# Retention on quarters of the PE array: chunks of 64 tokens, stages batched over 512

## The chip, the cores and the metric

One core of one Trainium2 chip. The time is the device time of one launch in microseconds (us), medians over runs in the undisturbed state. All times inside a kernel come from the profiled run and count from the start of its span, which is 1.7 to 2.2 us shorter than the device time. PE is TensorE, PEld its weight loads, DVE is VectorE, ACT ScalarE, POOL GpSimd, SP the engine that issues the DMAs.

## The reference

```python
def _attn_ref(q, k, v):            # (B, H, S, D) = (4, 8, 768, 64), fp32
    gamma = 1.0 - 2.0 ** (-5.0 - np.arange(H))
    for t in range(S):
        state = gamma * state + outer(k[:, :, t], v[:, :, t])     # D x D per head
        y[:, :, t] = q[:, :, t] @ state / sqrt(D)

def _moe_ref(x, w_in, w_out):      # x: 3072 x 512, w_in: 512 x 2048, w_out: 2048 x 512
    h = x @ w_in
    g = np.where(h > 0, h, np.exp(np.minimum(h, 0)) - 1)          # ELU
    return g @ w_out
```

Retention first, then a two-layer network over its output. The network is most of the work. The kernel runs it in blocks of 512 tokens: block 0 with plain products, blocks 1 to 5 with Strassen's seven products.

## The kernel before

Retention in chunks of 128 tokens. Within a chunk: scores (k times q under a causal mask), their product with v, the state's growth (k times v, summed in PSUM over the whole sequence), and the product of q with the state that came in. The decay sits in factors on v and on the output. For one chunk:

```python
def scores(m):
    qk, kv = raw[m]
    sc = [ps_s.tile([C, HP, C], FP32, name="sc", tag="s") for _ in range(2)]
    for p in range(HP):
        for a in range(2):
            r = slice(a * D, (a + 1) * D)
            nc.tensor.matmul(sc[a][:, p, :], lhsT=qk[r, 1, p, :], rhs=qk[r, 0, p, :], start=True, stop=True)
    # ... VectorE: pt = sc * mask

def values(m, ps=None):
    # y  = v, pt   : 8 matmuls, 128 x 64 of the array, 128 columns
    # kv += k, v   : 8 matmuls, 128 x 64, 64 columns
    # y += state, q: 8 matmuls, 64 x 64, 128 columns
    # ... VectorE: xb = y * etab;  ScalarE: state = kv * scale
```

While block tb runs its second layer, the four chunks of block tb + 1 are put between its products, one at a time:

```python
for j in range(4):
    s = next(cur)                    # one Strassen product: 32 PE records
    scale_v(m + j + 1) if j < 3 else None
    values(m + j)
    load(m + j + 2)
    if j < 3:
        scores(m + j + 1)
```

Weights come as float64 and are decoded on the chip during block 0. ScalarE takes the absolute value of the high word into a buffer of its own; VectorE works on it while ScalarE copies the low word (their first pair starts at 20.93 and 20.79 us):

```python
c = t4.tile([P, 1024], U32, name="wc", tag="t4")
nc.scalar.activation(cf, hi.bitcast(FP32), AF.Abs)
vec.tensor_scalar(...)  ; vec.tensor_scalar(...)  ; vec.scalar_tensor_tensor(...)
nc.scalar.activation(flat, lo, AF.Copy, scale=2.0**-29)
vec.tensor_tensor(out=flat, in0=c, in1=flat, op=ALU.add)
```

The ELU needs an intermediate tile r with two buffers: relu and exp on ScalarE, the last step on VectorE, which frees r.

## Time and profile before

| stage of the profiled run | us |
|---|---|
| to the first dense matmul (block 0's retention) | 25.5 |
| first plain layer, block 0 | 56.7 |
| second plain layer, block 0, with block 1's retention between | 71.3 |
| Strassen: up to block 1's first second-layer product | 45.1 |
| the rest | 505.0 |
| span | 703.6 |

The stages are read from the starts of the first matmul of each in PE's timeline (25.46, 82.16, 153.46, 198.59). The first plain layer holds one window of 3.41 us at half clock (26.57 to 29.98), which costs about 1.7 us (half of 3.41): its first line takes 8.80 us, the others 7.03. The median time was 704.22 us. The lines that carry the argument are in the prediction.

### The profile page before, as it was taken

The numbers are of one execution on the slowest core, as the hardware profiler recorded it, in microseconds if no ns is written. First come the engines' busy times: TensorE is split into PE (matmuls) and PEld (weight loads), VectorE is DVE, ScalarE is ACT, GpSimd is POOL, SyncE is SP. The second block draws the span as 40 slices with busy tenths as digits, with TensorE's granted clock in tenths as the row PEclk, the third lists the DMA queues.
The fourth block names the chain that finished last, engine by engine and source line by source line (L and its number), as shares of the span: only waits on it lengthen the run. The fifth ranks groups of instructions, "written<-read, shape, count | busy, mean of one in ns | idle before, by whom it ended". The sixth has DMA issues, their size and how long they took to land.

```text
span 703.6 us, 9258 instructions
## 1 busy us (share of the span) xinstructions
PE 681.0 (97%) x3904; PEld 541.9 (77%) x3904; DVE 314.3 (45%) x501; ACT 213.8 (30%) x356; POOL 24.2 (3%) x28
## 2 busy tenths in 40 slices
PE   6899999999999999999999999999999999999997
PEld 5444444468888888888888888788888878888886
DVE  4676798863435204445212454412343620354410
ACT  5656522214530003441001552000453000254100
POOL 0000000100000010000100000010000010000000
PEclk9999999999999999999999999999999999999999
DMA  8546568737014663003675002657101453400341
GB/s 335 203 143 248 206 206 291 272 119 249 1 60 136 219 199 106 0 1 104 211 228 176 0 1 61 193 187 222 58 0 49 146 181 88 137 0 1 102 153 46
DMA packets 51929, 93.92 MB, mean 133 GB/s; under 512 B 2224, under 2 KB 39088, under 8 KB 49840
## 3 DMA queue, kind: packets, MB, share of 16 engines
q1 hardware_dynamic: 51888, 93.33, 39.9%
q8 instruction: 31, 0.51, 0.3%
q14 instruction: 10, 0.08, 0.0%
HBM read 78.64 MB, written 14.68 MB: 133 GB/s over the span
## 4 chain that ended last, share of the span: by engine, by line
PE 92%; DVE 5%; DMA 1%; issue 0%; SPq 0%; ACT 0%; DVEq 0%; ACTq 0%
PE ps L430 35%; PE ps L394 34%; PE hp L296 8%; PE op L312 5%; PE sc L208 4%; PE y L231 3%; DMA qk<-in_qkv_dram 1%; PE y L251 1%; PE kv L241 1%; DVE w_s L333 1%; DVE wc L128 1%; DVE xb L256 1%; DVE pt L211 1%; DVE so L317 1%; DVE wo L130 1%
## 5 line engine op out<-in xcount | busy, mean ns | idle before, releaser
L430 PE MATMUL ps<-g,ws 128*128 128x256 f32 x1120 | 248.3, 381 | 0.7 <-ACT m L346 0.7
L430 PEld LDWEIGHTS ps<-g,ws 128*128 128x128 f32 x1120 | 211.1, 190 | 31.6 <-ACT m L346 1.1
L351 DVE TENSOR_TENSOR h<-ps,m 128x512 f32<-128x512 f32 x75 | 51.9, 692 | 253.5 <-ACT m L346 117.2
L346 ACT COPY m<-ps 128x512 f32<-128x512 f32 x75 | 43.2, 577 | 204.2 <-PE ps L430 117.9
L394 PE MATMUL ps<-xt,w_b 128*128 128x256 f32 x320 | 75.7, 379 | 0.0
L394 PE MATMUL ps<-xb,w_a 128*128 128x256 f32 x320 | 72.4, 379 | 0.0
L394 PE MATMUL ps<-xt,w_s 128*128 128x256 f32 x320 | 72.4, 379 | 0.0
L394 PEld LDWEIGHTS ps<-xt,w_b 128*128 128x128 f32 x320 | 60.7, 190 | 8.4 <-ACT m L346 0.2
L394 PEld LDWEIGHTS ps<-xt,w_s 128*128 128x128 f32 x320 | 60.7, 190 | 8.4 <-issue 0.2
L394 PEld LDWEIGHTS ps<-xb,w_a 128*128 128x128 f32 x320 | 60.7, 190 | 8.4 <-issue 0.2
L285 ACT ACTIVATE r<-r 128x512 f32<-128x512 f32 x96 | 60.5, 630 | 3.0
L312 PE MATMUL op<-g,wo 128*128 128x512 f32 x128 | 57.0, 598 | 3.0 <-DVE wo L130 3.0
L284 ACT ACTIVATE r<-h 128x512 f32<-128x512 f32 x60 | 37.8, 630 | 62.7 <-DVE h L351 62.7
L312 PEld LDWEIGHTS op<-g,wo 128*128 128x128 f32 x128 | 23.7, 190 | 31.4 <-issue 27.3
L287 DVE SCALAR_TENSOR_TENSOR g<-r,h 128x512 f32<-128x512 f32 x60 | 41.1, 686 | 15.2 <-ACT r L285 15.2
L208 PE MATMUL sc<-qk 64*128 64x128 f32 x384 | 33.3, 300 | 11.7 <-DMA qk<-in_qkv_dram 6.5
L208 PEld LDWEIGHTS sc<-qk 64*128 64x128 f32 x384 | 28.2, 198 | 19.5 <-DVE xb L256 7.6
L211 DVE TENSOR_TENSOR pt<-sc,cmask 128x512 f32<-128x512 f32 x48 | 30.9, 685 | 23.8 <-PE sc L208 23.6
L195 POOL TENSOR_TENSOR kvn<-kvn,vf 128x512 f32<-128x512 f32 x20 | 22.6, 1130 | 550.4 <-DMA kvn<-in_qkv_dram 470.8
L262 ACT ACTIVATE state<-kv 128x256 f32<-128x256 f32 x20 | 7.7, 383 | 109.3 <-PE kv L241 109.3
L256 DVE TENSOR_TENSOR xb<-y,etab 128x256 f32<-128x256 f32 x48 | 18.4, 420 | 47.8 <-PE y L251 40.8
L394 PE MATMUL ps<-xb,w_s 128*128 128x256 f32 x160 | 37.8, 379 | 0.0
(58 smaller groups left out, 467.1 us busy)
## 6 DMA issues: line engine op xcount, KB each, us to landing
ws<-scratch_dram SPq DMA_DIRECT2D x35, 1024.0 KB, 5.8
wraw<-in_w_dram SPq DMA_DIRECT2D x16, 1024.0 KB, 4.8
qk<-in_qkv_dram SPq DMA_DIRECT2D x24, 512.0 KB, 6.6
kvn<-in_qkv_dram SPq DMA_DIRECT2D x24, 512.0 KB, 7.4
out_dram<-h SPq DMA_DIRECT2D x20, 256.0 KB, 5.8
scratch_dram<-wo SPq DMA_DIRECT2D x8, 512.0 KB, 5.9
scratch_dram<-so SPq DMA_DIRECT2D x8, 512.0 KB, 2.8
out_dram<-ot SPq DMA_DIRECT2D x4, 256.0 KB, 6.5
```

What stands on the lines that cost most here:

```text
L208: nc.tensor.matmul(sc[a][:, p, :], lhsT=qk[r, 1, p, :], rhs=qk[r, 0, p, :], start=True, stop=True)
L211: nc.vector.tensor_tensor(out=pt[:, a], in0=sc[a], in1=cmask.unsqueeze(1).to_broadcast([C, HP, C]), op=ALU.mult)
L256: nc.vector.tensor_tensor(out=xb[:, 2 * a : 2 * a + 2, cc * C : (cc + 1) * C], in0=y[a], in1=etab[:, a, :, i * C : (i + 1) * C], op=ALU.mult,)
L284: nc.scalar.activation(r, h, AF.Relu, scale=-1.0)
L285: nc.scalar.activation(r, r, AF.Exp, scale=-1.0)
L287: later.append(lambda: nc.vector.scalar_tensor_tensor(g, r, -1.0, h, ALU.add, ALU.max))
L296: nc.tensor.matmul(hp, lhsT=w[n][:, j // 2, fi, j % 2, :], rhs=xb[:, j, :], start=(j == 0), stop=(j == 3))
L312: nc.tensor.matmul(ops[d], lhsT=wo[:, row, d * P : (d + 1) * P], rhs=gs[row * NF + f], start=(f == 0 and row == 0), stop=(f == NF - 1 and ...
L346: nc.scalar.copy(m, ps)
L351: nc.vector.tensor_tensor(out=h, in0=ps, in1=m, op=ALU.add)
L394: nc.tensor.matmul(ps[:, fi, :], lhsT=w[:, fi, j2, :], rhs=x[:, j2, :], start=(begin and fi == 0 and j2 == 0), stop=(j2 == 1), skip_group_ ...
L430: nc.tensor.matmul(ps[:, d, :], lhsT=ws[:, f, d * P : (d + 1) * P], rhs=gqs[f // 2][name][:, f % 2, :], start=(begin and f == 0 and d == 0 ...
```

## The change

The intent: with chunks of 64 tokens half of each score square is not computed, and with every operand 64 x 64, four matmuls are to run on four quarters of the array at once (in the kernel before, 64 x 64 records started four at a time, 6.7 ns apart). Stages are batched over 512 tokens, so that small tiles come between dense products less often (about 0.39 us each time, by the prediction's estimate from the trace); the states, no longer summed in PSUM, are added on VectorE. To make room, weights are decoded in place, the pool t4 falls from five buffers to four, the loads come four at a time, and Strassen's PSUM banks are four for five. The core of the diff:

```diff
+    def scores(tb, pp):
+        for x, qk in enumerate(two):
             for p in range(HP):
+                for sub in range(2):
+                    for a in range(2):
+                        nc.tensor.matmul(sc[a][rows(sub), x, p, :], lhsT=qk[rows(a), 1, p, rows(sub)],
+                                         rhs=qk[rows(a), 0, p, rows(sub)], ...)
...
+    def outputs(tb, pp):            # a generator: 32 matmuls v, pt and the half of q, state that
+        ...                         # goes to the same PSUM bank from the same rows;
+        yield                       # the other half after a pause
@@ decode
-        c = t4.tile([P, 1024], U32, name="wc", tag="t4")
-        cf = c.bitcast(FP32)
+        nc.scalar.activation(flat, lo, AF.Copy, scale=2.0**-29)
+
+        c, cf = lo, lo.bitcast(FP32)
         nc.scalar.activation(cf, hi.bitcast(FP32), AF.Abs)
...
-        nc.scalar.activation(flat, lo, AF.Copy, scale=2.0**-29)
@@ block 0's second layer
+        elif n == 6:
+            outputs_rest()
+            for m in range(2 * CPB, 3 * CPB):
+                load(m)
+                scale_v(m)
+            combine_w_in(3)
@@ block tb, second layer
+        next(cur)                                   # product 2
+            scores(tb + 1, 0); scores(tb + 1, 1)
+        next(cur)                                   # product 6
+            states(tb + 1, 0); states(tb + 1, 1)
+        next(cur)                                   # product 7
+            outputs_first(tb + 1)
+        assert next(cur) == "gap"                   # product 5
+            outputs_rest()
```

(combine_w_in for three of four parts moves into the first plain layer.)

More of the change, by code (lines that the diff above doesn't have):

```diff
@@ L63 @@
     const = ctx.enter_context(tc.tile_pool(name="const", bufs=1))
-    ldpool = ctx.enter_context(tc.tile_pool(name="ldpool", bufs=2))
+    ldpool = ctx.enter_context(tc.tile_pool(name="ldpool", bufs=4))
     stage = ctx.enter_context(tc.tile_pool(name="stage", bufs=3))
-    t4 = ctx.enter_context(tc.tile_pool(name="t4", bufs=5))
-    spool = ctx.enter_context(tc.tile_pool(name="spool", bufs=2))
-    xpool = ctx.enter_context(tc.tile_pool(name="xpool", bufs=1))
+    t4 = ctx.enter_context(tc.tile_pool(name="t4", bufs=4))
     mpool = ctx.enter_context(tc.tile_pool(name="mpool", bufs=4))
@@ L71, with load @@
     epool = ctx.enter_context(tc.tile_pool(name="epool", bufs=2))
-    ps_s = ctx.enter_context(tc.tile_pool(name="ps_s", bufs=2, space=PSUM))
-    ps_c = ctx.enter_context(tc.tile_pool(name="ps_c", bufs=1, space=PSUM))
-    ps_f = ctx.enter_context(tc.tile_pool(name="ps_f", bufs=5, space=PSUM))
+    gpool = ctx.enter_context(tc.tile_pool(name="gpool", bufs=20))
+    ps_r = ctx.enter_context(tc.tile_pool(name="ps_r", bufs=4, space=PSUM))
+    ps_f = ctx.enter_context(tc.tile_pool(name="ps_f", bufs=1, space=PSUM))
     chunks = [divmod(m, NCH) for m in range(NCHUNK)]
     raw = {}
-    def load(m, pool=None):
-        if m >= NCHUNK or m in raw:
+    def load(m):
+        if m >= NCHUNK:
             return
-        pool = pool or ldpool
-        qk = pool.tile([P, 2, HP, C], FP32, name="qk", tag="qk")
+        qk = ldpool.tile([P, 2, HP, C], FP32, name="qk", tag="qk")
         nc.sync.dma_start(qk.rearrange("p a h c -> p (a h c)"), qkv[m, :, 0:1024])
-        kv = pool.tile([C, 2, H, D], FP32, name="kvn", tag="kvn")
+        kv = ldpool.tile([C, 2, H, D], FP32, name="kvn", tag="kvn")
         nc.sync.dma_start(kv.rearrange("p a h c -> p (a h c)"), qkv[m, :, 1024:2048])
@@ L132, in decode @@
         load_piece()
-    startup = tc.tile_pool(name="startup", bufs=CPB)
-    start_pool = startup.__enter__()
-    load(0, start_pool)
-    load(1, start_pool)
+    load(0)
+    load(1)
     load_piece()
-    load(2, start_pool)
-    load(3, start_pool)
+    load(2)
+    load(3)
     load_piece()
     load_piece()
-    cmask = const.tile([P, P], FP32, name="cmask")
-    nc.gpsimd.memset(cmask, 0.0)
+    causal = t4.tile([P, P], FP32, name="causal", tag="t4")
+    nc.gpsimd.memset(causal, 0.0)
     nc.gpsimd.affine_select(
-        out=cmask, in_=cmask, compare_op=ALU.is_gt, fill=scale, base=0, pattern=[[-1, P]], channel_multiplier=1
+        out=causal, in_=causal, compare_op=ALU.is_gt, fill=1.0, base=0, pattern=[[-1, P]], channel_multiplier=1
     )
+    cmask = const.tile([P, D], FP32, name="cmask")
+    for sub in range(2):
+        r = slice(sub * D, (sub + 1) * D)
+        nc.vector.tensor_copy(cmask[r, :], causal[r, r])
     pos_s = const.tile([P, NCH, H], I32, name="pos_s")
@@ L162 @@
     nc.scalar.activation(vf, vf, AF.Exp, scale=-1.0)
+    nc.vector.tensor_scalar(vf, vf, scale, None, ALU.mult)
     head = lambda a, u, c: 2 * (2 * u + c) + a
@@ L182 @@
     xt = [const.tile([P, 2, TH], FP32, name=f"xt{n}") for n in range(4)]
-    act, held = {}, {}
+    carry = [const.tile([P, HP, D], FP32, name=f"carry{n}") for n in range(2)]
+    held = {}
     def scale_v(m):
@@ L189, in scale_v @@
         qk, kv = raw[m]
-        if 0 < m < CPB:
+        if m in (1, 3):
             for h in range(H):
@@ L197, in scale_v @@
         )
-    def scores(m):
-        if m >= NCHUNK:
-            return
-        qk, kv = raw[m]
-        sc = [ps_s.tile([C, HP, C], FP32, name="sc", tag="s") for _ in range(2)]
-        for p in range(HP):
-            for a in range(2):
-                r = slice(a * D, (a + 1) * D)
-                nc.tensor.matmul(sc[a][:, p, :], lhsT=qk[r, 1, p, :], rhs=qk[r, 0, p, :], start=True, stop=True)
-        pt = t4.tile([C, 2, HP, C], FP32, name="pt", tag="t4")
-        for a in range(2):
-            nc.vector.tensor_tensor(
-                out=pt[:, a], in0=sc[a], in1=cmask.unsqueeze(1).to_broadcast([C, HP, C]), op=ALU.mult
-            )
-        act[m] = pt
@@ L216, in values @@
-    def values(m, ps=None):
-        if m >= NCHUNK:
-            return
-        ps, tag = (ps, "f") if ps else (ps_s, "s")
-        i = chunks[m][1]
-        (qk, kv), pt = raw[m], act.pop(m)
-        raw[m] = None
-        kn, vn = kv[:, 0], kv[:, 1]
-        cc = m % CPB
-        y = [ps.tile([P, 2, C], FP32, name="y", tag=tag) for _ in range(2)]
-        for a in range(2):
-            for u in range(2):
-                for c in range(2):
-                    h, p = head(a, u, c), 2 * u + c
-                    nc.tensor.matmul(
-                        y[a][c * D : (c + 1) * D, u, :], lhsT=vn[:, h, :], rhs=pt[:, a, p, :],
-                        start=(u == 0), stop=(i == 0), skip_group_check=True,
-                    )
-        if i == 0:
-            held["kv"] = ps_c.tile([P, HP, D], FP32, name="kv", tag="kv")
-        if i < NCH - 1:
-            for p in range(HP):
-                for a in range(2):
-                    h = 2 * p + a
-                    nc.tensor.matmul(
-                        held["kv"][a * D : (a + 1) * D, p, :], lhsT=kn[:, h, :], rhs=vn[:, h, :],
-                        start=(i == 0 and p == 0), stop=(i == NCH - 2), skip_group_check=True,
-                    )
-        if i > 0:
-            st = held["state"]
-            for u in range(2):
-                for a in range(2):
-                    for c in range(2):
-                        r, p = slice(a * D, (a + 1) * D), 2 * u + c
@@ new lines, with state, fresh @@
+    rows = lambda n: slice(n * D, (n + 1) * D)
+    def state(tb, n):
+        if n % (2 * CPB) == 0:
+            return carry[(tb + n // (2 * CPB)) % 2]
+        return xt[n // 2].rearrange("p a t -> p (a t)")[:, (n % 2) * 256 : (n % 2 + 1) * 256].rearrange(
+            "p (h e) -> p h e", e=D
+        )
+    def fresh(tb, n):
+        return (tb * 2 * CPB + n) % (S // D) == 0
+    def scores(tb, pp):
+        two = [raw[tb * CPB + 2 * pp + x][0] for x in range(2)]
+        sc = [ps_r.tile([P, 2, HP, D], FP32, name="sc", tag="r") for _ in range(2)]
+        for x, qk in enumerate(two):
+            for p in range(HP):
+                for sub in range(2):
+                    for a in range(2):
@@ L251, in values @@
                         nc.tensor.matmul(
-                            y[a][c * D : (c + 1) * D, u, :], lhsT=st[r, p, :], rhs=qk[r, 0, p, :],
-                            start=False, stop=True, skip_group_check=True,
+                            sc[a][rows(sub), x, p, :], lhsT=qk[rows(a), 1, p, rows(sub)],
+                            rhs=qk[rows(a), 0, p, rows(sub)], start=True, stop=True, skip_group_check=True,
                         )
@@ L256, in values @@
             nc.vector.tensor_tensor(
-                out=xb[:, 2 * a : 2 * a + 2, cc * C : (cc + 1) * C], in0=y[a],
-                in1=etab[:, a, :, i * C : (i + 1) * C], op=ALU.mult,
-            )
-        if i < NCH - 1:
-            held["state"] = spool.tile([P, HP, D], FP32, name="state", tag="state")
-            nc.scalar.activation(held["state"], held["kv"], AF.Copy, scale=scale)
+                out=two[a][:, 1].rearrange("p h c -> p (h c)").rearrange("p (n t) -> p n t", t=D),
+                in0=sc[a].rearrange("p x h t -> p (x h) t"),
@@ new lines, in scores, with states @@
+                in1=cmask.unsqueeze(1).to_broadcast([P, 2 * HP, D]), op=ALU.mult,
+            )
+    def states(tb, pp):
+        kvs = [ps_r.tile([P, 2, HP, D], FP32, name="kv", tag="r") for _ in range(2)]
+        order = [(x, sub) for x in range(2) for sub in range(2)]
+        last = lambda x, sub: fresh(tb, 4 * pp + 2 * x + sub + 1)
+        for x in range(2):
+            kv = raw[tb * CPB + 2 * pp + x][1]
+            for p in range(HP):
+                for sub in range(2):
+                    for a in range(2):
+                        if not last(x, sub):
+                            nc.tensor.matmul(
+                                kvs[sub][rows(a), x, p, :], lhsT=kv[rows(sub), 0, 2 * p + a, :],
+                                rhs=kv[rows(sub), 1, 2 * p + a, :], start=True, stop=True, skip_group_check=True,
+                            )
+        for x, sub in order:
+            n = 4 * pp + 2 * x + sub
+            if last(x, sub):
+                continue
+            if fresh(tb, n):
+                nc.scalar.copy(state(tb, n + 1), kvs[sub][:, x])
+            else:
+                nc.vector.tensor_tensor(out=state(tb, n + 1), in0=kvs[sub][:, x], in1=state(tb, n), op=ALU.add)
@@ new lines, in outputs @@
+    def outputs(tb, pp):
+        y = [ps_r.tile([P, 2 * 2, 2, D], FP32, name="y", tag="r") for _ in range(2)]
+        for x in range(2):
+            kv = raw[tb * CPB + 2 * pp + x][1]
+            for j in range(4):
+                a, u = divmod(j, 2)
+                pt = raw[tb * CPB + 2 * pp + a][0][:, 1].rearrange("p h c -> p (h c)")
+                for sub in range(2):
+                    for c in range(2):
+                        p = 2 * u + c
+                        nc.tensor.matmul(
+                            y[sub][rows(c), j, x, :], lhsT=kv[rows(sub), 1, head(a, u, c), :],
+                            rhs=pt[rows(sub), (x * HP + p) * D : (x * HP + p + 1) * D],
+                            start=(x == 0 and j == 0), stop=False, skip_group_check=True,
+                        )
+        for other in range(2):
+            if other:
+                for sub in range(2):
+                    seen = epool.tile([P, 8], FP32, name="seen", tag="seen")
+                    nc.vector.tensor_copy(seen.rearrange("p (j x) -> p j x", x=2), y[sub][:, :, :, 0])
+                yield
+            for x in range(2):
+                q = raw[tb * CPB + 2 * pp + x][0]
+                for u in range(2):
+                    for a in range(2):
+                        sub = a ^ other
+                        n = 4 * pp + 2 * x + sub
+                        if fresh(tb, n):
+                            continue
+                        for c in range(2):
+                            p = 2 * u + c
+                            nc.tensor.matmul(
+                                y[sub][rows(c), 2 * a + u, x, :], lhsT=state(tb, n)[rows(a), p, :],
+                                rhs=q[rows(a), 0, p, rows(sub)], start=False, stop=True, skip_group_check=True,
+                            )
+        i = chunks[tb * CPB + 2 * pp][1]
+        for sub in range(2):
+            place = lambda t: t.rearrange("p j (x s c) -> p j x s c", x=2, s=2)[:, :, :, sub, :]
+            nc.vector.tensor_tensor(
+                out=place(xb[:, :, 2 * pp * C : 2 * (pp + 1) * C]), in0=y[sub],
+                in1=place(etab.rearrange("p a u t -> p (a u) t")[:, :, i * C : (i + 2) * C]), op=ALU.mult,
+            )
@@ L264, with outputs_first, outputs_rest @@
+    def outputs_first(tb):
+        held["y"] = [outputs(tb, pp) for pp in range(2)]
+        for g in held["y"]:
+            next(g)
+    def outputs_rest():
+        for g in held.pop("y"):
+            for _ in g:
+                pass
     half = [slice(0, TH), slice(TH, TB)]
@@ L293, in plain_first @@
                 for fi in range(2):
-                    hp = ps_f.tile([P, TB], FP32, name="hp", tag="f")
+                    hp = ps_r.tile([P, TB], FP32, name="hp", tag="r")
                     for j in range(4):
@@ L305, in plain_second @@
     def plain_second(gs):
-        ops = [ps_f.tile([P, TB], FP32, name="op", tag="f") for _ in range(4)]
+        ops = [bank(x).rearrange("p a b -> p (a b)") for x in "aabd"]
         for f in range(NF):
@@ L339, in combine_w_in, with bank @@
         tt(s4, a12, s2, ALU.subtract)
-    def bank():
-        return ps_f.tile([P, 2, TH], FP32, name="ps", tag="f")
+    def bank(x):
+        return ps_f.tile([P, 2, TH], FP32, name="p" + x, tag=x, bufs=2 if x == "a" else 1)
     def kept(ps):
@@ L357, in strassen @@
         yield
-        pa = bank()
+        pa = bank("a")
         product(1, pa, True)
@@ L361, in strassen @@
         yield
-        pb = bank()
+        pb = bank("b")
         product(2, pb, True)
@@ L368, in strassen @@
         yield
-        pd = bank()
+        pd = bank("d")
         product(7, pd, True)
@@ L455, in second @@
         return strassen(product, use, None)
-    for j in range(CPB + 1):
-        if j < CPB:
-            scale_v(j)
-            scores(j)
-        if j > 0:
-            if j == CPB:
-                decode()
-            values(j - 1, ps_f)
+    for pp in range(2):
+        scale_v(2 * pp)
+        scale_v(2 * pp + 1)
+        scores(0, pp)
+        states(0, pp)
+        if pp == 0:
+            decode()
+    outputs_first(0)
+    outputs_rest()
     decode()
-    startup.__exit__(None, None, None)
-    gpool = ctx.enter_context(tc.tile_pool(name="gpool", bufs=20))
     gs = {}
@@ L472 @@
             decode()
-        if n == 4:
-            load(CPB)
-        if n == 8:
-            load(CPB + 1)
+        if n in (3, 5, 7, 9):
+            load(CPB + (n - 3) // 2)
+        if n in (7, 11, 15):
+            combine_w_in((n - 7) // 4)
+    for m in range(CPB, 2 * CPB):
+        scale_v(m)
     for n, _ in enumerate(plain_second(gs)):
         decode()
-        m, at = CPB + n // 2, n % 2
-        if at == 0:
-            scale_v(m)
-            scores(m)
-            combine_w_in(n // 2)
-        else:
-            values(m)
-            load(m + 2)
+        if n == 1:
+            scores(1, 0)
+            scores(1, 1)
+        elif n == 3:
+            states(1, 0)
+            states(1, 1)
+        elif n == 5:
+            outputs_first(1)
+        elif n == 6:
+            outputs_rest()
+            for m in range(2 * CPB, 3 * CPB):
+                load(m)
+                scale_v(m)
+            combine_w_in(3)
     combine_x()
@@ L506 @@
         cur = second(tb, gqs)
+        more = tb + 1 < NTB
         next(cur)
@@ L511 @@
         flush()
-        m = (tb + 1) * CPB
-        scale_v(m)
-        scores(m)
-        for j in range(4):
-            s = next(cur)
-            scale_v(m + j + 1) if j < 3 else None
-            values(m + j)
-            load(m + j + 2)
-            if j < 3:
-                scores(m + j + 1)
-        assert s == "gap"
+        next(cur)
+        if more:
+            scores(tb + 1, 0)
+            scores(tb + 1, 1)
+        next(cur)
+        if more:
+            states(tb + 1, 0)
+            states(tb + 1, 1)
+        next(cur)
+        if more:
+            outputs_first(tb + 1)
+        assert next(cur) == "gap"
+        if more:
+            outputs_rest()
+            for m in range((tb + 2) * CPB, (tb + 3) * CPB):
+                load(m)
+                scale_v(m)
         for _ in cur:
             pass
-        combine_x() if tb + 1 < NTB else None
+        combine_x() if more else None
         tail = iter(())
```

## The prediction

The sum of the forecast is whole: 704.2 - 25.4 - 3.6 + 1.5 = 676.7, each term from the trace of the kernel before. The ranges (681, 680 to 685, 668 to 694) are as recorded.

> **What bounds the kernel now.** I read the page's busy shares first, then the chain that ended last, then the timeline of one block of 512 tokens, and last the groups by line.
>
> ```profile
> PE 681.0 (97%) x3904; PEld 541.9 (77%) x3904; DVE 314.3 (45%) x501; ACT 213.8 (30%) x356; POOL 24.2 (3%) x28
> ...
> PE 92%; DVE 5%; DMA 1%; issue 0%; SPq 0%; ACT 0%; DVEq 0%; ACTq 0%
> PE ps L430 35%; PE ps L394 34%; PE hp L296 8%; PE op L312 5%; PE sc L208 4%; PE y L231 3%; DMA qk<-in_qkv_dram 1%; PE y L251 1%; PE kv L241 1%; DVE w_s L333 1%; DVE wc L128 1%; DVE xb L256 1%; DVE pt L211 1%; DVE so L317 1%; DVE wo L130 1%
> ```
>
> PE is the bound, and nearly the whole chain is PE. L430, L394, L296 and L312 are the dense layers, which the change leaves alone; sc, y and kv (L208, L231, L241, L251) are the retention. Busy time misleads here, because a record's duration overlaps its neighbours'. I therefore read starts in the timeline of PE, one block:
>
> ```profile
> 209.04 1.16 PE L208 MATMUL sc<-qk 64*128 64x128 f32 x16
> 210.13 7.17 PE L430 MATMUL ps<-g,ws 128*128 128x256 f32 x32
> 217.24 1.09 PE L231 MATMUL y<-pt,kvn 128*64 128x128 f32 x16
> 218.16 0.64 PE L241 MATMUL kv<-kvn 128*64 128x64 f32 x16
> 218.72 0.67 PE L251 MATMUL y<-qk,state 64*64 64x128 f32 x16
> 219.91 1.49 PE L208 MATMUL sc<-qk 64*128 64x128 f32 x16 [0.51 <-DVE xb L256]
> 221.32 7.17 PE L430 MATMUL ps<-g,ws 128*128 128x256 f32 x32
> ...
> 252.43 0.48 PE L430 MATMUL ps<-g,ws 128*128 128x256 f32 x1
> ```
>
> The reader is to see two things. Retention sits between the dense products and PE does nothing else meanwhile, so each of its microseconds is a microsecond of the span. And each matmul of the program leaves two records (8 become x16). Undisturbed, a dense product of 32 records takes 6.91 us (311.24 to 318.14, and again where nothing lies between), 216 ns a record. From 209.04 to 252.43 are 43.39 us, with four such products: 43.39 - 4 x 6.91 = 15.75 us of retention. The same sum gives 14.84, 14.37 and 15.75 for the later three blocks that prepare a next one: **60.7 us** in all. The block prepared during plain_second lies between 82.16 and 153.46: 71.3 - 8 x 6.87 = 16.3 us over, of which 3.0 are waits for decoded weights:
>
> ```profile
> L312 PE MATMUL op<-g,wo 128*128 128x512 f32 x128 | 57.0, 598 | 3.0 <-DVE wo L130 3.0
> ```
>
> **The rate of small matmuls.** Single records in time order go in waves. Score records (64x128 of the array, 128 columns) start in pairs 5 to 7 ns apart, one pair per 109 ns; y records (128x64, 128 columns) likewise, a pair per 109. kv records (128x64, 64 columns): a pair per 58 ns. Inter-chunk y records (64x64, 128 columns): four at a time, 6.7 ns apart, every 109 ns. So a wave lasts as long as its columns stream (109 ns for 128, 58 for 64) and every independent piece of the array gets one record in it. Per 128 tokens the stream is 8 x 109 (scores) + 8 x 109 (y) + 8 x 58 (kv) + 4 x 109 (inter) = 2.6 us. The rest of a block's 15 us is switching and waiting. An isolated score group delays the next dense product by 1.18 us, and that product's first interval is 320 ns instead of 216: 1.28 us for 8 x 0.11 = 0.89 of streaming, so **about 0.39 us per insertion**.
>
> [...] kv averages 58/2 = 29 ns a record and inter 109/4 = 27[...], yet neighbours start 6.7 ns apart. This is the main doubt below. [...] So decoding in place, with step 2, should cost what it does: L126 and L127 690 ns, L128 1228, L130 1225 to 1305. No run shows step 2 yet.
>
> **The change part by part.**
> (1) Scores. Chunks of 64 drop half of the score square: 16 matmuls of 64 columns per 128 tokens, in four pieces. 32 records / 4 = 8 waves x 58 = 0.47 us for 0.87.
> (2) Inside-chunk outputs: the same, 0.47 for 0.87.
> (3) States: twice as many, on quarters: 8 waves x 58 = 0.47, as before.
> (4) Inter-chunk: twice as many of half the columns: 8 x 58 = 0.47 for 0.44.
> Together 32 waves = 1.86 us per 128 tokens for 2.6, or 7.4 us a block for 10.5.
> (5) Batching. A block now has four insertions (scores; states; outputs with the first half of inter; its second half), one after each of four dense products: 4 x 0.39 = 1.6 us. Before there were some sixteen changes of mode a block, and waits such as the 0.51 above. A block costs 7.4 + 1.6 = 9.0, about 8.8 with the states dropped where a sequence starts. Four blocks: 35.3 for 60.7, so **-25.4 us**.
> (6) VectorE: per block 4 masks at 0.69 and 4 output scalings at about 0.7, as much as before (8 x 0.69, 8 x 0.42) or less, and up to 8 state additions at 0.42, chained, some 4 us. They are due only after the next dense product (6.9 us), where VectorE also has 4 x 0.69 of subtractions; it fits with 1 to 2 us to spare. Hidden.
> (7) plain_second. combine_w_in moves partly into plain_first, where VectorE has 1.8 us free in each 7.06 us; the move fits but delays the first decode here. Walking it through with 2.3 us of ScalarE and 3.85 of VectorE per decode, 1.7 for the four "so" operations, a slot freed by the product before last, and 8.8 of retention, I get waits of 2.5 us at the second step, 0.5 at the fourth and 1.2 at the sixth. 55 + 8.8 + 4 = 67.7 for 71.3: **-3.6 us**.
> (8) Start. Before, the first dense matmul begins at 25.46. Now the first decode lies between the two pairs on VectorE, ahead of the second pair's masks, states and outputs. From the last kv arrival (17.24) and the decode's end (about 18.5) I count scaling, two masks, four chained additions, the seen copies and four output scalings: about 27.0, **+1.5 us**.
> (9) Dense PSUM banks, four for five. The tight one is pd: in the trace C21 is read out at 182.21 and the next product that needs that bank begins at 183.05, so it fits. DMA moves the same bytes, earlier than needed.
> Sum: 704.2 - 25.4 - 3.6 + 1.5 = **676.7, say 677 us**.
>
> **The rivals.**
> (a) **A floor per matmul for the whole engine.** [...] For: no stretch before averages under 27 ns. Against: the 6.7 ns spacing, and 8 matmuls dispatched within 0.13 us between two semaphore records at 13.46 and 13.59, 16 ns a matmul where four pieces need 29.
> (b) **Instruction supply.** The quarters need 128 record pairs per 128 tokens for 64, up to 138 instructions per us where before the densest stretch had about 40. The page counts 31 instruction packets of 16 KB, each taking 0.9 to 2.0 us. [...] the groups starve now and then: up to 1 us a block, 681.
> (c) **VectorE becomes the bound** in plain_second or in the start, because [...] chains meet: 3 to 8 us, 680 to 685.
> (d) The batched second half of the outputs waits for the seen copies, or states come late for outputs_first: at most 1 us a block.
>
> **Range and chances.** 677 is the sum with full waves and no new waits. Downward there is little: cheaper insertions (0.3 us instead of 0.39) and no waits in plain_second give about 670. Upward (b), (c) and (d) together give up to 690[...]. I give (a) in full force one chance in eight. Eight in ten: 668 to 694. Faster by over 2% means under 690.1: 0.81; within 2%: 0.16; slower: 0.03, for a clash that I don't see.
>
> **What would show it.** In PE's timeline of a block: four insertions, score and state groups of 128 records (112 where a sequence starts) lasting about 1.9 us from first to last start, outputs 2.8, the rest 0.9; the first dense product of a block's four to the fifth, less 27.6 us, about 9 (15.75 before). Starts of single records: waves of four, 58 ns apart[...]. Mean of L126's successor at 0.69 us[...]. First hp record near 27, plain_second 67.7 long. PE idle inside the blocks near zero. Wrong would make me: waves that don't overlap four-fold, or gaps within the groups without a named releaser.

## The result, and the profile after

712.33 us, against 704.22 before: the ratio is 1.0106 (95%: 1.0074 to 1.0138). A ratio here is the mean time of one kernel's fast runs over that of the other's of the same rounds, so not quite the ratio of the medians. No gain, where 4% was predicted. The busy line and the chain on the page of the changed kernel:

```profile
PE 665.5 (94%) x5440; PEld 530.1 (75%) x5440; DVE 319.9 (45%) x521; ACT 207.9 (29%) x332; POOL 24.8 (4%) x28
...
PE 81%; DVE 7%; DMA 4%; ACT 3%; issue 3%; SPq 1%; DVEq 0%; ACTq 0%
```

PE is idle for 6% of the span in place of 3%, and its share of the chain fell from 92 to 81%. DVE, DMA, ACT and "issue" took its place: new waits. By stages, in us:

| stage | before | after | difference | predicted |
|---|---|---|---|---|
| to the first dense matmul | 25.5 | 32.4 | +6.9 | +1.5 |
| first plain layer | 56.7 | 60.2 | +3.5 | 0 |
| second plain layer | 71.3 | 71.5 | +0.2 | -3.6 |
| Strassen, to the second layer | 45.1 | 54.2 | +9.1 | 0 |
| the rest, with four blocks of retention | 505.0 | 490.4 | -14.6 | -25.4 |
| span | 703.6 | 708.7 | +5.1 | -27.5 |

**The blocks.** PE's timeline of the changed kernel for the block that before took 15.75 us of retention (start, duration, instructions, idle time before them):

```profile
235.65 2.10 PE L225 MATMUL sc<-qk 64*64 64x64 f32 x128
237.68 7.17 PE L481 MATMUL pa<-g,ws 128*128 128x256 f32 x32
244.78 2.08 PE L247 MATMUL kv<-kvn 64*64 64x64 f32 x112
246.79 7.17 PE L481 MATMUL pd<-g,ws 128*128 128x256 f32 x32
253.90 1.16 PE L271 MATMUL y<-qk,kvn 64*64 64x64 f32 x64
...
255.35 1.13 PE L271 MATMUL y<-qk,kvn 64*64 64x64 f32 x64
256.28 0.40 PE L293 MATMUL y<-qk,xt 64*64 64x64 f32 x12
259.04 0.90 PE L293 MATMUL y<-qk,xt 64*64 64x64 f32 x20 [2.36 <-issue]
259.87 8.41 PE L481 MATMUL pa<-g,ws 128*128 128x256 f32 x32
...
269.30 7.17 PE L481 MATMUL pa<-g,ws 128*128 128x256 f32 x32
```

The score group has the predicted length: 128 records, 2.03 us to the next product. Single records start four at a time, 6.5 ns apart, and the waves 58 ns apart (236.519, .526, .532, .539; .577, ...). But in the middle of the outputs PE stops for 2.36 us, "issue", that is, with no releaser in the profile, and the dense product behind the gap takes 8.41 us for 7.17. I measure a block's retention from the start of product 2 to that of product 4, less five products of 6.91: 13.1, 8.9, 10.8 and 12.9 us, 45.7 in sum. The second block has no gap and costs what was predicted (about 8.8). The windows around the gap (busy PE, its instructions, granted clock, DMA share, GB/s) tell why 8.41:

```profile
252.00:255.40 3.40, 3.40 (x110) 1.00 0.07 17
256.60:259.00 2.40, 0.08 (x4) 1.00 0.85 296
259.10:262.40 3.30, 3.30 (x26) 0.50 0.04 11
262.60:266.00 3.40, 3.40 (x18) 1.00 0.00 0
```

After the gap the granted clock is 0.5 for one window of 3.4 us: about 1.7 us (half of the 3.41 us in the clock records) lost on top of 2.36. The gaps of 2.36 us (here) and 2.11 us (fourth block, 583.26 to 586.67) were followed by such a window, the one of 1.62 us, in the third block, was not. Length alone does not decide in these runs: the run x_r3, described below, has a gap of 2.39 us with no half clock behind it.

```profile
577.23 0.38 PE L271 MATMUL y<-qk,kvn 64*64 64x64 f32 x9 [2.39 <-issue]
...
578.01 7.17 PE L481 MATMUL pa<-g,ws 128*128 128x256 f32 x32
```

**The first plain layer.** From 60.53 on PE waits before each pair of products for the ELU, which has to empty their PSUM banks:

```profile
60.53 7.10 PE L347 MATMUL hp<-xb,w_a 128*128 128x512 f32 x16 [0.46 <-DVE g L338]
68.65 7.30 PE L347 MATMUL hp<-xb,w_b 128*128 128x512 f32 x16 [1.02 <-DVE g L338]
```

A pair of products takes 8.1 us for the 6.87 that PE needs. In this run the half-clock window of the start (26.88 to 30.29) ends before the layer begins, so 60.2 is to be set against 55.0 before (56.7 less the 1.7 of half clock). Five other runs with this layer unchanged (x_pad42, x_split, x_late, x_burst3, x_start) took 62.3 to 63.2 us, with a half-clock window inside it. **The second plain layer** waits 4.34 us for the decoded weights of its second step, and two half-clock windows (101.97 to 108.80) begin during that wait. **The hand-over to Strassen** (PE, then two instructions of SP's queue, then DVE):

```profile
173.06 3.78 PE L445 MATMUL pb<-xb,w_a 128*128 128x256 f32 x8 [7.12 <-ACT ot L380]
```

```profile
160.53 0.39 SPq L87 DMA_DIRECT2D kvn<-in_qkv_dram  x1
161.09 0.34 SPq L374 DMA_DIRECT2D scratch_dram<-wo  x1
```

```profile
173.68 0.69 DVE L380 COPY ot<-pd 128x512 f32<-128x512 f32 x1 [8.75 <-DMA scratch_dram<-so]
```

PE waits for PSUM to be emptied, the emptying waits for a buffer, the buffer for the last scratch writes, and these were issued behind 4 MB of loads. Again two half-clock windows (170.24 to 177.07) begin during the wait.

### The profile page after: what moved, and what is told of

Same layout as the page of the kernel before. It is cut to its first block, busy times and chain, and to the rows that moved or that the text cites. A ratio compares the mean times of both kernels' runs of the same rounds, so it can differ in the third digit from the quotient of the medians.

```text
span 708.7 us, 12361 instructions
## 1 busy us (share of the span) xinstructions
PE 665.5 (94%) x5440; PEld 530.1 (75%) x5440; DVE 319.9 (45%) x521; ACT 207.9 (29%) x332; POOL 24.8 (4%) x28
## 4 chain that ended last, share of the span: by engine, by line
PE 81%; DVE 7%; DMA 4%; ACT 3%; issue 3%; SPq 1%; DVEq 0%; ACTq 0%
PE pa L481 20%; PE pa L445 19%; PE pd L481 10%; PE pd L445 9%; PE pb L445 5%; PE pb L481 5%; PE pa L363 3%; PE y L271 2%; DMA kvn<-in_qkv_dram 2%; PE y L293 2%; PE kv L247 2%; DMA scratch_dram<-wo 2%; DVE wraw L128 2%; PE sc L225 1%; PE pb L363 1%
## 5 line engine op out<-in xcount | busy, mean ns | idle before, releaser
L481 PE MATMUL pa<-g,ws 128*128 128x256 f32 x640 | 145.9, 387 | 2.3 <-issue 1.6
L481 PEld LDWEIGHTS pa<-g,ws 128*128 128x128 f32 x640 | 122.6, 193 | 20.5 <-issue 2.0
L397 ACT COPY m<-pa 128x512 f32<-128x512 f32 x75 | 43.3, 577 | 268.8 <-PE pa L481 184.4
L481 PE MATMUL pd<-g,ws 128*128 128x256 f32 x320 | 71.1, 380 | 0.0
L481 PEld LDWEIGHTS pd<-g,ws 128*128 128x128 f32 x320 | 60.5, 190 | 8.3
L445 PE MATMUL pb<-xb,w_a 128*128 128x256 f32 x160 | 39.7, 393 | 7.1 <-ACT ot L380 7.1
L445 PEld LDWEIGHTS pb<-xb,w_a 128*128 128x128 f32 x160 | 31.4, 197 | 12.0 <-ACT ot L380 7.5
L445 PE MATMUL pa<-xt,w_b 128*128 128x256 f32 x160 | 38.0, 380 | 0.6 <-ACT m L397 0.6
L445 PE MATMUL pa<-xt,w_s 128*128 128x256 f32 x160 | 38.0, 380 | 0.0
L445 PE MATMUL pd<-xt,w_b 128*128 128x256 f32 x160 | 37.8, 379 | 0.0
L445 PE MATMUL pa<-xb,w_a 128*128 128x256 f32 x160 | 37.8, 379 | 0.0
L363 PE MATMUL pa<-g,wo 128*128 128x512 f32 x64 | 32.6, 634 | 4.8 <-DVE wo L129 4.8
L481 PE MATMUL pb<-g,ws 128*128 128x256 f32 x160 | 35.3, 379 | 0.0
```

Source lines behind the costliest of these rows:

```text
L363: nc.tensor.matmul(ops[d], lhsT=wo[:, row, d * P : (d + 1) * P], rhs=gs[row * NF + f], start=(f == 0 and row == 0), stop=(f == NF - 1 and ...
L397: nc.scalar.copy(m, ps)
L445: nc.tensor.matmul(ps[:, fi, :], lhsT=w[:, fi, j2, :], rhs=x[:, j2, :], start=(begin and fi == 0 and j2 == 0), stop=(j2 == 1), skip_group_ ...
L481: nc.tensor.matmul(ps[:, d, :], lhsT=ws[:, f, d * P : (d + 1) * P], rhs=gqs[f // 2][name][:, f % 2, :], start=(begin and f == 0 and d == 0 ...
```

## The experiments

All experiments gave the reference's result. Each changes one thing in the changed kernel, except where more is named. They ran in three rounds on different chips, and in each the kernel before ran beside them: 705.48 us (x_pad42, x_split, x_late, x_r3), 706.12 (x_burst3, x_abs5, x_start, x_best1) and 705.05 (x_best2, x_dec16). The changed kernel was not run again, so ratios to the kernel before are the sounder comparison: 1.0106 for the changed kernel. Runs called "one look" have one execution, whose state is unknown; their stages, not their times, carry the argument.

**Is the gap a wait for instructions?** (x_pad42) I counted PE's records in order, weight loads and the semaphore waits between them included. The four gaps with no releaser (one in the start, three in the blocks) come after record 705, 4033, 7873 and 9665. Modulo 256 that is 193 each time. The profile page lists 43 instruction packets for the DMA queue q8, 0.70 MB, 16 KB each. PE has 10,978 records in the trace, 255 for each of them (before: 7,890 over 31, 254.5 each), and 256 is the largest step that fits the four places. So I take a packet for 256 of PE's instructions, an estimate from these counts. In all four cases a packet is in flight or begins within the gap, and PE goes on 1.3 to 1.4 us after its end. The output groups (384 instructions, fewer where a sequence starts) that had a gap in or just behind them met the first such boundary after 91, 126 and 48 instructions, the one without a gap after 204. My theory was that a group starves if a boundary falls in its first third, so that a second packet is needed before it has come. So I added work that shifts the boundaries:

```diff
+    extra = [ps_r.tile([P, 2, HP, D], FP32, name="extra", tag="r") for _ in range(2)]
+    for k in range(42):
+        c, a = k % 2, k // 2 % 2
+        nc.tensor.matmul(extra[a][rows(c), 0, 0, :], lhsT=etab[rows(a), 0, 0, 0:D],
+                         rhs=etab[rows(a), 0, 0, 0:D], start=True, stop=True, skip_group_check=True)
     combine_x()
```

> The changed kernel with 42 useless 64x64 matmuls (168 PE instructions, results never read) added once, between the plain and the Strassen part. Theory: the gaps of 1.6 to 2.4 us inside the output groups are waits for PE's next packet of 256 instructions (all lie at the same place modulo 256). A group of 384 starves when a packet boundary falls some 45 to 130 instructions after its start; it does so in blocks 1, 3, 4 (91, 126, 48), not in block 2 (204). Adding 168 moves the boundaries to about 179, 36, 214, 136: no gap left inside the blocks, or a short one in block 4. Each block's retention near 8.8 us (before: 13.0, 8.8, 10.7, 12.8), the time 702 to 705 in place of 712, although work was added. Rival (the gaps are waits for data or PSUM that the profile fails to name): the same three gaps stay and the time is 712 to 714.

Measured: 708.46 us, ratio to before 1.0036 (1.0006 to 1.0065). The blocks took 8.9, 8.9, 8.9 and 14.0 us. Added, useless work made the kernel some 4 us faster (the intervals of the two ratios do not meet), but not by the 7 to 10 us expected. PE's timeline of the padded kernel, the same block as above:

```profile
255.60 1.16 PE L271 MATMUL y<-qk,kvn 64*64 64x64 f32 x64
...
257.05 1.13 PE L271 MATMUL y<-qk,kvn 64*64 64x64 f32 x64
257.98 0.67 PE L293 MATMUL y<-qk,xt 64*64 64x64 f32 x32
258.58 7.17 PE L481 MATMUL pa<-g,ws 128*128 128x256 f32 x32
```

The same instructions, no gap, the dense product at 7.17 again. The gaps in blocks 1 and 3 are gone as foretold. In block 4, where I had put the boundary on the edge (no gap, "or a short one"), a gap remained just behind the group, and it was longer than I had allowed for, 3.5 us between starts; it lies after record 9921, 193 modulo 256 once more. A wait for data would not move with 168 useless instructions.

**Without any place modulo 256.** (x_split) The output group in three pieces, none over 256 instructions:

```diff
-            outputs_first(tb + 1)
+            ys = [outputs(tb + 1, pp) for pp in range(2)]
+            next(ys[0])                       # after product 7
         assert next(cur) == "gap"
-            outputs_rest()
+            next(ys[1])                       # after product 5
+            for _ in ys[0]: pass
+        next(cur)                             # product 3
+            for _ in ys[1]: pass
```

> The changed kernel with the output group of each block in three pieces (first pair of chunks after product 7, second pair and the first pair's rest after product 5, the second pair's rest after product 3), none over 256 instructions. Theory of instruction supply: no gap inside a group whatever its place modulo 256, one more insertion of 0.39 us a block: blocks near 9.2 us for 45.3 in sum now, time 703 to 706. Rival (waits for data): the pieces come later, so gaps shrink a little but stay; time 709 to 712.

Measured: 703.37 us, ratio 0.9964 (0.9942 to 0.9986). All four blocks cost 9.1 us, 36.4 in sum for 45.7, no gap in any. The expectation held. The gap in the start, which this run leaves alone, stayed (2.44 us).

**How many instructions are at hand, how fast is the supply?** (x_burst3) The scores issued three times over:

```diff
-        for x, qk in enumerate(two):
+        for x, qk in [y for y in enumerate(two) for _ in range(3 if tb > 1 else 1)]:
```

> The changed kernel with each block's score matmuls (blocks 2 to 5) issued three times over into the same place: groups of 768 PE instructions instead of 256, result unchanged. Theory: [...] a new packet of 256 takes some 4.3 us from the moment its predecessor is used up, so the first 300 to 500 instructions run at wave speed (58 ns for 8), then two gaps of 2 to 2.5 us lie 256 instructions apart, at the same place modulo 256 as before; the group lasts 9 to 11 us from first to last start in place of 5.6. Rival (the gaps in the output groups belong to waits for VectorE or PSUM): three times 1.87 = 5.6 us without a gap.

Measured (one look): 748.74 us, state unknown as for any single run. PE's timeline of the first such group:

```profile
236.51 3.49 PE L225 MATMUL sc<-qk 64*64 64x64 f32 x224
244.68 4.58 PE L225 MATMUL sc<-qk 64*64 64x64 f32 x160 [4.68 <-issue]
```

The group runs for 448 instructions (224 records, each with its weight load) and stops; the count is 193 modulo 256. The number and the length of the gaps were not as I expected: one of 4.5 to 4.9 us between starts in three blocks, and two of 1.6 and 2.1 us in one; the groups lasted 12.5, 9.3, 12.1 and 12.0 us (9 to 11 expected). In the three blocks a half clock follows the gap; why no second gap came there was not shown.

The other three groups first stopped after 338, 484 and 406 instructions, again at 193 modulo 256. So no fixed number is at hand: each of these groups went through the rest of one packet and the whole next one. And the supply had no fixed rate. From the first instruction of a packet to the first of the next, 3.5 to 6.8 us passed at these stops, and 4.2 to 6.1 at the four gaps of the changed kernel: 38 to 74 instructions per us, where waves of quarters use 8 per 58 ns, 138 per us. The trace's DMA records show which part varies. In the changed kernel's first block the next packet began 1.96 us after the first instruction of its predecessor, in the fourth 0.74 us after it. The windows between the two moments (last two columns: DMA share, GB/s):

```profile
254.55:256.50 1.95, 1.95 (x144) 1.00 0.62 147
578.29:579.03 0.74, 0.74 (x64) 1.00 0.00 0
```

The same holds at all 46 stops of over 0.75 us at a packet boundary in the runs, each after record 193 modulo 256: where the DMA engines moved next to no other data (share up to 0.06) the packet began 0.6 to 1.1 us after that moment, where their share was 0.95 or more 1.7 to 4.4 us after it. Whether the data traffic is the cause was not shown: no experiment varied it alone.

**The hand-over.** (x_late) The loads moved behind block 0's last output:

```diff
             outputs_rest()
-            for m in range(2 * CPB, 3 * CPB):
-                load(m)
-                scale_v(m)
             combine_w_in(3)
+    for m in range(2 * CPB, 3 * CPB):
+        load(m)
+        scale_v(m)
     combine_x()
```

> The changed kernel with the 4 MB of loads for block 2 issued after the plain part's output instead of before its last weight writes. Theory: in the changed kernel these loads lie ahead of the last scratch writes in the DMA queue, the output tiles wait for those writes to land (8.8 and 10.2 us), the PSUM banks stay full and PE waits 7.1 us before the second product of the Strassen part, and then runs two 3.4 us windows at half clock. Expected: that wait under 1 us, 1.5 to 3.4 us of slow clock gone, time 702 to 705. Rival (the output tiles wait for the four-buffer ring whatever the loads do): the wait stays above 4 us, time above 708.

Measured: 702.08 us, ratio 0.9964 (0.9941 to 0.9987). The Strassen stage before the second layer took 46.0 us for 54.2:

```profile
164.85 1.89 PE L445 MATMUL pa<-xb,w_a 128*128 128x256 f32 x8
166.58 1.89 PE L445 MATMUL pb<-xb,w_a 128*128 128x256 f32 x8
169.24 1.97 PE L445 MATMUL pa<-xt,w_s 128*128 128x256 f32 x8 [0.78 <-DVE xt L318]
```

The 7.12 us and the half clock are gone; 0.78 us remain for another operand. It was the order of the DMA queue. (The gaps of the blocks stay in this run: 3.0, 1.5 and 1.7 us.)

**The first plain layer.** (x_r3) A third buffer for r:

```diff
-        r = epool.tile([P, 512], FP32, name="r", tag="r")
+        r = epool.tile([P, 512], FP32, name="r", tag="r", bufs=3)
```

> The changed kernel with three buffers in place of two for the ELU's intermediate tile. Theory: in the first plain layer a loop of ScalarE and VectorE, closed by those two buffers, sets the pace: relu, exp, then the decode's two ScalarE operations one after the other before VectorE's four, then the ELU's last step that frees a buffer, 8.15 us for two products where PE needs 6.87 (it was 7.06 before, where VectorE began after one of the two). A third buffer opens the loop: the layer takes 55 to 57 us for 60.2, the waits of PE for g vanish, and the next layer's 4.3 us wait for its first decoded weight shrinks too: time 704 to 709. Rival (VectorE's own load sets the pace): the layer stays at 60, time 712.

Measured: 701.85 us, ratio 0.9951 (0.9916 to 0.9986); the layer took 55.0 us for 60.2, the next 69.3 for 71.5. The layer is as expected, the time is below the 704 to 709 expected: the stages of the profiled run (703.86 us) account for 7 us of gain, two of the other runs were 4 us faster, and why is open. PE in that layer, without waits:

```profile
59.39 7.03 PE L347 MATMUL hp<-xb,w_a 128*128 128x512 f32 x16
66.25 7.03 PE L347 MATMUL hp<-xb,w_b 128*128 128x512 f32 x16
```

The cross-check (x_abs5) undid the decode in place (working copy in t4, absolute value first; five buffers in t4, three in mpool) and kept two buffers for r:

> The changed kernel with the decode as it was: a buffer of its own for the working copy, the absolute value first and the low word's copy last, beside VectorE (five buffers in that pool, three of the PSUM copies' pool to make room). Theory: the first plain layer's loop is back at 7.06 us a pair of products instead of 8.15, so that layer takes 56.5 to 57.5 us for 60.2 to 62.5, with two buffers for the ELU's intermediate. Rival (the layer is slow because combine_w_in moved into it): it stays above 59.

Measured (one look): 703.16 us; the layer took 56.4 us, a half-clock window included. So either end of the loop mends it, and the move of combine_w_in is not what slowed the layer. In the kernel before, too, ScalarE waited for the ELU's last step on VectorE in every pair (2.6 us), and a pair took 7.06 us. The loop in the changed kernel, from ACT's and DVE's timelines:

```profile
53.49 1.12 ACT L121 ACTIVATE w_a<-wraw 128x1024 uint32<-128x1024 uint32 x1
54.65 1.15 ACT L124 ACTIVATE wraw<-wraw 128x1024 f32<-128x1024 f32 x1
```

```profile
55.82 0.70 DVE L126 TENSOR_SCALAR wraw<-wraw 128x1024 f32<-128x1024 f32 x1 [3.00 <-ACT wraw L124]
```

Working in place, ScalarE must copy the low word out before it may overwrite it, so VectorE begins 1.1 us later. VectorE's own operations, two of them now with step 2 in source and destination, cost what they did (L126 693 ns, L127 697, L128 1226, L129 1225).

**The second plain layer.** (x_dec16) The second output weight decoded two products earlier, on top of the third buffer for r (in the loop of the first plain layer):

```diff
-        if n % 2 == 0 and n < 14:
+        if n % 2 == 0 and n < 16:
             decode()
```

> The changed kernel with the third ELU buffer and the second output weights decoded two products earlier, in the first plain layer, and nothing else. Theory: the wait of PE for the decoded weights before the second step of the second plain layer (4.3 us in the changed kernel, 3.0 with the third buffer alone, then a half clock) arises because combine_w_in's 2.8 us stand ahead of that decode on VectorE; with the decode done earlier the wait is gone and that layer takes 63 to 65 us for 69.3. Rival (the ring of four buffers delays it): it stays at 68 or more.

Measured (one look): 698.96 us. That layer took 63.8 us for 69.3, as expected. But the stage behind it grew from 54.8 to 56.8: part of what was won went to the wait for the scratch writes, still in place there (8.8 us for 7.6, and one half-clock window more). The wait removed upstream was not worth its full length (5.5 us won, 2.0 lost again), because the next one was still there.

**The start.** (x_start) The first pair of chunks finished before the second begins:

```diff
         states(0, pp)
+        for _ in outputs(0, pp):
+            pass
         if pp == 0:
             decode()
-    outputs_first(0)
-    outputs_rest()
     decode()
```

> The changed kernel with the first pair of chunks of block 0 finished (outputs too) before the second pair begins, so that its 256 output instructions run while the second pair's loads are still on their way. Theory: at the start 1.4 us are a later landing of the last load, and about 2.6 us a packet gap and 1 to 2 us the half clock after it; with the output group cut in two the gap falls into time that is spent waiting anyway: first dense product at 28 to 29.5 us for 31 to 32.4, time 708 to 710. Rival (the start is set by loads and the scaling of v on ScalarE): it stays at 31 or later.

Measured: 711.21 us, ratio 1.0072 (1.0056 to 1.0088); the first dense matmul at 31.4 us. The expectation (28 to 29.5) failed. PE, then DVE, of that run:

```profile
23.03 1.99 PE L247 MATMUL kv<-kvn 64*64 64x64 f32 x64 [4.47 <-issue]
```

```profile
21.10 1.23 DVE L129 CUSTOM_DVE_ANT_0 w_a<-wraw,w_a 128x2048 uint16<-128x2048 uint16 x1
22.25 0.68 DVE L199 TENSOR_TENSOR kvn<-kvn,vf 128x512 f32<-128x512 f32 x1
```

This "issue" is not an instruction gap: its record is 102 modulo 256, and PE begins 0.1 us after VectorE has scaled v, an operation that stood behind the decode, which itself stood behind the first pair's output. The profile names no releaser in both cases; the count tells them apart. Two shorter gaps of this start are of the other kind: 1.1 us at 16.6 and 0.8 us at 29.3, both at 193 modulo 256. A group of 256 is no safeguard here, where small groups follow one another without long instructions between them; the last version below still has two (1.6 and 0.5 us).

**All together.** The three single changes that gained (x_split, x_late, x_r3), the earlier decode and the start (x_best1):

> All together: late loads (-9), three ELU buffers and the first output weights decoded one step earlier (-10 to -13), output groups of at most 256 instructions (-9), the two halves of block 0 one after the other (-2 to -3). Sum 679 to 684 us for 712, 3% below the kernel before. If the gains overlap (a wait taken away only uncovers the next), 690 or more.

Measured: 680.80 us, ratio 0.9639 (0.9622 to 0.9656). The gains add up. Then the start once more, with the decode and the scaling ahead of the first pair's output scaling (x_best2; against the kernel after, the guard on the loop's own scale_v and the changes of x_best1 cut):

```diff
+        y = outputs(0, pp)
+        next(y)
         if pp == 0:
             decode()
+            scale_v(2)
+            scale_v(3)
+        for _ in y:
+            pass
```

> The combined kernel with one thing changed in the start: VectorE decodes the first weights and scales the third chunk's v right after the first pair's seen copies, ahead of the first pair's output scaling, so that the second pair's states no longer wait for the decode (in the combined kernel they started at 23.5 us, 0.1 us after VectorE's scaling, which stood behind 3.8 us of decode). Expected: first dense product at 29 to 30 us for 31.3, time 679 to 680 for 680.8. Rival (the last load and the half clock set the start): it stays at 31.

Measured: 676.55 us, ratio 0.9606 (0.9581 to 0.9631), with the first dense matmul at 28.2 us (29 to 30 expected). It gained more than expected: half of the difference between the profiled runs, 3.1 us, is the start, the other half the first plain layer (55.0 for 58.1 us), because two half-clock windows that lay in it are gone. The page:

```profile
PE 655.5 (97%) x5440; PEld 526.3 (78%) x5440; DVE 319.2 (47%) x521; ACT 208.2 (31%) x332; POOL 24.0 (4%) x28
...
PE 94%; DVE 2%; DMA 1%; issue 1%; ACT 0%; SPq 0%; DVEq 0%
```

PE's share of the chain is 94%, above the kernel before. The stages are 28.2, 55.0, 63.8, 46.0 and 480.4 us. This version beats both kernels.

## Why the prediction was wrong

It said 677 us and the changed kernel took 712.33. By stages (profiled runs, table above) the miss of 32.6 us is 10.8 in the blocks of retention, 9.1 at the hand-over, 5.4 in the start, 3.8 and 3.5 in the two plain layers. The steps, in its own numbering:

- **Steps 1 to 4, the waves: right.** Four records per wave, 58 ns a wave, in every undisturbed group; rival (a), a floor per matmul for the whole engine, did not come at more than 14.5 ns: four records start per 58 ns.
- **Step 5, "A block costs 7.4 + 1.6 = 9.0, about 8.8": right for a block without a gap** (8.9 in block 2, and in three blocks of the padded kernel; 9.1 with one more insertion). The total, "-25.4 us", failed: the blocks took 45.7 us for 35.3. The term that was mis-sized is **rival (b), "up to 1 us a block"**. It named the kind of wait that the counts and x_pad42 then showed. Measured against 8.9, it cost 4.2, 0, 1.9 and 4.0 us, some 10 in all. I had allowed for a short late packet. What I left out is the turnaround, 4.2 to 6.1 us for 256 instructions that a group uses up in 1.9, and the half clock that followed two of the three gaps. The comparison behind it ("about 40" instructions per us before) set an average against a peak: by the prediction's own waves, four records with their weight loads per 109 ns were already 73 per us, though only for short stretches.
- **Step 6, VectorE's additions hidden: right.** No wait of PE for states or masks of 0.4 us or more shows within the blocks.
- **Step 7, the decode: the durations right, the order missed.** (Its sum is slightly off too: the three waits add to 4.2, the whole to 68.0.) "combine_w_in moves partly into plain_first, where VectorE has 1.8 us free in each 7.06 us; the move fits": it fits by load, but 7.06 was a loop through two buffers of r, not a load, and the in-place decode, which I had weighed for its stride alone, put 1.1 us of ScalarE into it. Cost: 5.2 us (60.2 against 55.0 with the loop open). In the next layer I foresaw 2.5 us of wait at the second step, and 4.3 came, with two half-clock windows: 71.5 us in place of 67.7. With the decode done in time 63.8 is possible, better than I had it.
- **Step 8, the start: "about 27.0" was 32.4.** I placed the decode right and missed what came with it: a packet gap of 2.6 us between records in the middle of the outputs, a half-clock window, and a last load that landed some 1.4 us later (18.7 for 17.2). The first two can be eased by order: 28.2 in the last version, where the load landed at 19.2. It came between 17.7 and 18.7 in two runs with the same start; why it lands later than before was not tested and stays open.
- **Step 9, "DMA moves the same bytes, earlier than needed": this sentence cost 8.2 us.** It looked at when loads are needed, and not at what stands behind them in the queue. The four banks for five, the point that I did check, were indeed enough in the Strassen loop, but for 0.6 us of waiting in sum.
- **Rival (c)** named VectorE as a possible bound in the second plain layer and the start. The operations that now have step 2 took 693 and 697 ns (690 and 694 before). Chains that meet is what the 4.3 us behind combine_w_in and, in x_start, the decode ahead of the second pair's scaling were.

With the unforeseen waits taken away 676.55 us were measured, for 676.7 predicted. That agreement is partly luck: the start is 1.2 us above my 27.0, the second plain layer 3.9 below my 67.7, the first 1.7 below the 56.7 that I had left as it was, and each block has one more insertion.

## What to carry to other kernels

Here smaller instructions asked more of what feeds the engine (138 per us in the waves, where 42 to 61 per us came at the four gaps of the changed kernel): count instructions per microsecond as well as work, keep dense groups short, with long instructions in between (here 256 instructions went through without a gap between dense products, 384 did so only at lucky places), and suspect the supply where gaps without a releaser recur at the same count modulo a fixed number (here 193 modulo 256). When buffers are saved by working in place or by batching loads, walk every loop that a small ring closes and every queue in which something now stands ahead of something urgent. And where several waits were added at once, take away each alone first, then all together: the three that mended one whole wait won 9 to 10.5 us each, the start alone 1, all repairs together 36 (712.33 to 676.55).
